# Seven block products in the output matmul of batches 2 to 6, with batch 2's products laid behind a plain chunk

## The chip, the cores and the metric

The kernel runs on one core of a Trainium2 chip. The metric is the device time of one execution in microseconds. Five engines matter: PE (TensorE, with its weight loads PEld), DVE (VectorE), ACT (ScalarE), POOL (GpSimd) and the DMA queues that SP, ACT and POOL issue to.

## The reference

Per batch and head, 32 packed rows `p` attend to `k`, `v`; then `q` attends to the packed result. The heads, side by side, are the input of a two-layer block with a cosine gate.

```python
def sm_attn(qq, kk, vv):
    s = scale * np.matmul(qq, kk.transpose(0, 1, 3, 2))
    a = np.exp(s - np.max(s, axis=-1, keepdims=True))
    a = a / (np.sum(a, axis=-1, keepdims=True) + 1e-09)
    return np.matmul(a, vv)
p_packed = sm_attn(p, k, v)             # 8 batches, 8 heads, 32 x 64
x = sm_attn(q, p_packed, p_packed)      # 8 batches, 8 heads, 576 x 64
h = x_rows @ w_in                       # 4608 x 512 @ 512 x 2048
out = (h * np.cos(h)) @ w_out           # 4608 x 2048 @ 2048 x 512
```

## The kernel before

It is a pipeline over batches. **Stage s** begins with the second attention's scores of batch s (`s2`) and lasts until those of batch s + 1. Its second part is a **slot** of 16 hidden-layer steps: four matmuls into a PSUM buffer (`psA`, three of them), a sine with bias pi/2 (so a cosine) on ACT, and the product `gT` on DVE, which gives the buffer back. Between all this, output matmuls of batch s - 1 are laid as **filler**, so that PE never waits. A batch's output has four chunks of 128 rows, and the last 64 rows of two batches make a joint chunk.

The names in the listings: `a1` holds the weights of the first attention, and a DMA transposes it to `a1T`; the **packed projection** (`pp`) multiplies `a1T` with V; the **weight product** (`PPW`) multiplies its result with `w_in`; a hidden-layer step multiplies `PPW` with `a2n`, the normalised weights of the second attention; `ot` is a PSUM buffer of the output matmuls.

```python
    def out_gen(b):                      # the filler: one matmul of 512 columns per step
        groups = [(0, 1), (2,), (3,)] if b == 0 else [(c,) for c in range(n_chunks(b))]
        for grp in groups:
            pss = {c: O.tile([128, DM], FP32, name="ot", tag="ot") for c in grp}
            ...
    for s in range(3, B):                # stage s (cut)
        fill(1000)
        set_filler(s - 1)
        if nxt:
            permute_v(s + 1)
        s2(s)
        ppw(s, 2, V)
        if nxt:
            xbar("q", s + 1)             # DMA transposes, in the order of SP's queue
        fill(10)
        if nxt:
            s1(s + 1)
            ppw(s, 3, V)
            a1_xbar(s + 1)               # transposes a1 of the next batch
            ...
        sums2(s, 1)
        normalise(s)
        fill(13)
        ...
        slot(s, [(5, lambda: pp(s + 1, engs=(ACT, ACT))), ...   # the packed projection: needs a1T
```

Only the last batch used a form with seven block products for two chunks, in `last_out`, with its partial results `o1` in the pool of V tiles (`vp`), which had two buffers.

The softmax here doesn't subtract the row's maximum and nothing guards it: scores larger than these inputs give would overflow.

## Time and profile before

247.05 us median of three runs (246.82 to 247.11). How long each stage lasts, read off PE's timeline from the first scores matmul of a stage to that of the next:

| stage | us before | filler in it |
|---|---|---|
| 2 | 25.75 | batch 1: 80 matmuls of 512 columns |
| 3 | 25.22 | batch 2: 64 |
| 4 | 28.42 | batch 3: 80 |
| 5 | 25.22 | batch 4: 64 |
| 6 | 28.35 | batch 5: 80 |

Sixteen matmuls at 0.216 us are 3.46 us; 28.42 - 25.22 is 3.2. So from stage 3 on a stage's length follows its count of filler, which is what a full PE looks like. Stage 2, laid out otherwise, is shorter than stage 4 with the same count.

### The profile page before, as it was taken

How to read it: one execution, taken by the hardware profiler on the slowest of the kernel's cores; microseconds unless marked ns; L12 is line 12 of the kernel's file. 1: busy time of each engine (PE TensorE's matmuls, PEld its weight loads, DVE VectorE, ACT ScalarE, POOL GpSimd, SP SyncE). 2: the span in 40 equal slices, each digit the busy share in tenths (PEclk: the TensorE clock that was granted, in tenths of full speed). 3: DMA queues.
4: the chain of work that ended last, by engine and by line, in shares of the span. 5: the costliest groups of instructions: out<-in, count | busy, mean ns of one | idle time of the engine just before them, and what ended most of it. 6: DMA issues, size and time to landing. Idle time of an engine off the chain costs nothing.

```text
span 245.3 us, 5164 instructions
## 1 busy us (share of the span) xinstructions
PE 235.1 (96%) x2061; PEld 134.2 (55%) x2061; DVE 171.0 (70%) x262; ACT 169.4 (69%) x283; POOL 84.7 (35%) x91
## 2 busy tenths in 40 slices
PE   8888799999999999999999999999999999999993
PEld 3454374566545654575446554565456554566682
DVE  2449987677667877678857666678667865788542
ACT  2359789877666887888876777887777774876000
POOL 8252543241310454005411305020529960099000
PEclk9999999999999999999999999999999999999999
DMA  6999999999899989998999994999381111301332
GB/s 89 202 203 206 204 207 227 201 241 156 179 189 186 199 171 217 224 203 135 220 196 202 155 232 83 178 172 200 82 169 43 43 45 43 86 3 44 84 88 86
DMA packets 64391, 37.36 MB, mean 152 GB/s; under 512 B 36880, under 2 KB 59920, under 8 KB 64368
## 3 DMA queue, kind: packets, MB, share of 16 engines
q0 software_dynamic: 23152, 18.75, 50.0%
q1 hardware_dynamic: 40784, 18.09, 35.4%
q8 instruction: 16, 0.26, 0.4%
q10 hardware_dynamic: 432, 0.20, 0.4%
q14 instruction: 7, 0.06, 0.1%
HBM read 37.22 MB, written 9.44 MB: 190 GB/s over the span
## 4 chain that ended last, share of the span: by engine, by line
PE 80%; DMA 11%; DVE 3%; ACT 3%; issue 1%; POOL 1%; DVEq 0%; POOLq 0%
PE ot L387 43%; PE psA L256 22%; DMA w_in_bf<-in_moe_w_in_dram 7%; PE ot L360 5%; DMA vbf<-in_v_dram 3%; PE psA L207 3%; DVE gT L263 2%; PE psA L129 2%; ACT cosT L260 2%; PE psA L183 2%; PE psA L233 1%; PE ot L370 1%; ACT ppT L75 1%; DVE vp L77 0%; PE psA L166 0%
## 5 line engine op out<-in xcount | busy, mean ns | idle before, releaser
L387 PE MATMUL ot<-w_out_bf,gT 128*128 128x512 bf16 x448 | 119.3, 380 | 0.0
L263 DVE TENSOR_TENSOR gT<-psA,cosT 128x576 bf16<-128x576 f32 x128 | 93.8, 756 | 28.6 <-ACT cosT L260 27.8
L260 ACT ACTIVATE cosT<-psA 128x576 bf16<-128x576 f32 x128 | 82.4, 652 | 24.6 <-PE psA L256 22.1
L256 PE MATMUL psA<-a2n,PPW 128*128 128x288 bf16 x512 | 83.8, 286 | 1.4 <-DVE gT L263 0.4
L256 PEld LDWEIGHTS <-PPW 128*128 128x128 bf16 x512 | 49.3, 98 | 34.8 <-issue 4.1
L387 PEld LDWEIGHTS <-gT 128*128 128x128 bf16 x448 | 41.6, 98 | 35.7 <-issue 6.5
L77 DVE CAST PPW<-psA 128x1024 bf16<-128x1024 f32 (+1 forms) x23 | 26.9, 1175 | 11.6 <-PE psA L207 11.5
L267 POOL COPY joint<-gT 128x512 bf16<-128x512 bf16 x16 | 10.0, 627 | 38.3 <-DVE gT L263 38.3
L77 POOL COPY vp<-vbf 96x3072 bf16<-96x3072 bf16 x7 | 19.3, 2750 | 6.3 <-DMA vbf<-in_v_dram 6.3
L243 DVE SCALAR_TENSOR_TENSOR a2n<-a2u,r,lns 128x576 bf16<-128x576 bf16 x16 | 12.3, 813 | 7.3 <-ACT lns L241 7.3
L235 ACT ACTIVATE lns<-psA 128x576 f32<-128x576 f32 x16 | 10.2, 650 | 7.1 <-PE psA L233 6.5
L140 ACT ACTIVATE a<-psA 128x576 bf16<-128x576 f32 x16 | 10.3, 647 | 6.7 <-PE psA L129 6.7
L77 DVE COPY osb<-ot 128x512 f32<-128x512 f32 x18 | 12.4, 691 | 2.1 <-PE ot L387 1.4
L387 PE MATMUL ot<-w_out_bf,joint 128*128 128x512 bf16 x48 | 13.0, 379 | 0.0
L225 ACT ACTIVATE a2u<-psA,rs 128x576 bf16<-128x576 f32 x16 | 11.0, 738 | 1.4 <-PE psA L129 1.3
L608 POOL COPY gate<-kT 1x1 bf16<-1x1 bf16 x3 | 0.5, 180 | 32.4 <-DMA kT<-kbf 32.4
L75 ACT CAST ppT<-psA 64x128 bf16<-64x128 f32 x24 | 6.2, 260 | 6.7 <-DVE ppT L77 5.9
L207 PE MATMUL psA<-w_in_bf,ppT 64*32 64x512 bf16 x224 | 10.1, 380 | 0.0
L425 PE MATMUL ot<-wz 128*128 128x512 bf16 x25 | 8.9, 496 | 1.2 <-DVE wz L436 1.2
L241 ACT ACTIVATE lns<-lns 128x576 f32<-128x576 f32 x16 | 10.0, 676 | 0.0
L314 POOL TENSOR_TENSOR S<-gT 128x256 bf16<-128x256 bf16 x8 | 5.4, 671 | 12.5 <-DVE gT L263 12.5
L84 POOL DMA_DIRECT2D vbf<-in_v_dram x8 | 6.2, 775 | 6.4 <-DVE vp L77 4.4
(94 smaller groups left out, 216.4 us busy)
## 6 DMA issues: line engine op xcount, KB each, us to landing
kbf<-in_k_dram POOLq DMA_DIRECT2D x8, 576.0 KB, 12.8
vbf<-in_v_dram POOLq DMA_DIRECT2D x8, 576.0 KB, 8.0
qbf<-in_q_dram POOLq DMA_DIRECT2D x8, 576.0 KB, 9.9
out_dram<-osb SPq DMA_DIRECT2D x22, 192.0 KB, 2.8
out_dram<-osb SPq DMA_DIRECT2D x24, 128.0 KB, 2.4
w_in_bf<-in_moe_w_in_dram POOLq DMA_DIRECT2D x4, 512.0 KB, 17.2
w_out_bf<-in_moe_w_out_dram POOLq DMA_DIRECT2D x4, 512.0 KB, 20.8
out_dram<-osb SPq DMA_DIRECT2D x22, 64.0 KB, 2.2
```

The source lines that it names most:

```text
L77: eng.tensor_copy(out=out, in_=in_)
L140: ACT.activation(out=a1[b % 2][:, y, :, 0:TP].rearrange("p (e m) x -> p e m x", e=2), in_=ps[y][:, :, 0:HS].rearrange("p e (m x) -> p e m ...
L207: nc.tensor.matmul(ps[y][32 * x:32 * x + 32, :], ppT[b % 2][r, 2 * x + y, :], w_in_bf[r, x, n * 512:(n + 1) * 512], start=True, stop=True)
L225: ACT.activation(out=a2u[b][:, y].rearrange("p (e x) -> p e x", e=2), in_=ps[y][:, :, 0:HS], func=AF.Exp, scale=rs1[b][:, y:y + 1])
L235: ACT.activation(out=lns[b][:, y].rearrange("p (e x) -> p e x", e=2), in_=ps[:, :, 0:HS], func=AF.Ln)
L241: ACT.activation(out=lns[b][:, y], in_=lns[b][:, y], func=AF.Exp, scale=-1.0)
L243: V.scalar_tensor_tensor(out=a2n[b][:, y], in0=a2u[b][:, y], scalar=r1[b][:, y:y + 1], in1=lns[b][:, y], op0=ALU.mult, op1=ALU.mult)
L256: nc.tensor.matmul(ps[:, e, 0:HS], PPW[b][:, y, fc * 128:(fc + 1) * 128], a2n[b][:, y, e * HS:(e + 1) * HS], start=(y == 0), stop=(y == 1))
L260: ACT.activation(out=csv, in_=ps[:, :, 0:HS], func=AF.Sin, bias=PI_HALF)
L263: V.tensor_tensor(out=gT[b][:, fc, :].rearrange("p (e x) -> p e x", e=2), in0=ps[:, :, 0:HS], in1=csv, op=ALU.mult)
L360: nc.tensor.matmul(ps[:, i], lhs[:, kp, :], rhs[:, kp, :], start=kp == 0, stop=kp == 7)
L387: nc.tensor.matmul(pss[c], w, w_out_bf[:, fc, :], start=(fc == 0), stop=(fc == NFC - 1))
```

## The change

The intent: fewer PE cycles. Chunks 0 and 1 of batches 2 to 6, seen as a 2 x 2 block matrix product, take seven block products (56 matmuls of 256 columns) and additions in place of eight (32 of 512). The sums of blocks of `gT` (`S`) are made on POOL in the slot, those of weight blocks (`T`) once, the last of them ahead of the loads of slot 2; DVE puts the products together from PSUM. The joint chunks are dealt as halves, one to each batch from 1 to 6. Batches 3 to 6 begin with the products; batch 2 has a plain chunk ahead of them. To make room, the pool of V tiles has one buffer in place of two.

```diff
-    vp_pool = ctx.enter_context(tc.tile_pool(name="vp", bufs=2))
+    vp_pool = ctx.enter_context(tc.tile_pool(name="vp", bufs=1))
...
+    def pair_gen(b, p):
... (operands cut)
+        def then2(ps):
+            plus(o1[:, 0:3:2, :], ps, m1)
+        def then7(ps):
+            plus(u3, ps[:, 0], o1[:, 2])
+            plus(o2[:, 0], ps[:, 1], u3)
+        def then5(ps):
+            plus(o2[:, 1], ps[:, 0], u3)
+            store(o2, 2 * p + 1)
+            plus(o1[:, 2], ps[:, 0], o1[:, 2])
+            plus(o1[:, 1], ps[:, 1], o1[:, 2])
+            store(o1, 2 * p)
+        for names, then in (((1,), lambda ps: copy(V, m1, ps[:, 0])), ((2, 6), then2), ((7, 4), then7), ((5, 3), then5)):
... (8 matmuls of 256 columns for each product)
+    def joints_of(b):
+        return [(b - (b + 1) % 2, (b + 1) % 2)] if 0 < b < B - 1 else []
...
     def out_gen(b):
+        joints = [joint_half(j, i, store_half(j)) for j, i in joints_of(b)]
+        if b == FIRST:                       # FIRST = 2
+            yield from direct_gen(b, ((2,),))
+            yield from pair_gen(b, 0)
+            yield from direct_gen(b, ((3,),))
+            for g in joints:
+                yield from g
+            return
+        if b > FIRST:
+            yield from pair_gen(b, 0)
+            for g in joints:
+                yield from g
+            yield from direct_gen(b, ((2,), (3,)))
+            return
...
+            elif s >= FIRST and fc in (7, 11, 15):
+                S_sums(s, 0, G, *{7: (0, 4), 11: (4, 6), 15: (6, 8)}[fc])
...
-            fill(quota - first if first != quota else quota)
+            fill_halves(quota - first if first != quota else quota)
```

Cut are: Ln and Exp left in PSUM from batch 3 on, the small scale on ACT, PPW in quarter tiles, and the last batch's second set of sums, moved between its additions.

## The prediction

> **What bounds the kernel now.** I read the page first: its busy shares, its tenths, and the chain that ended last.
>
> ```profile
> span 245.3 us, 5164 instructions
> PE 235.1 (96%) x2061; PEld 134.2 (55%) x2061; DVE 171.0 (70%) x262; ACT 169.4 (69%) x283; POOL 84.7 (35%) x91
> PE 80%; DMA 11%; DVE 3%; ACT 3%; issue 1%; POOL 1%; DVEq 0%; POOLq 0%
> ```
>
> PE is named in both. A busy share alone proves little, because a matmul's recorded time holds its latency. So I asked the waits view for PE alone from 96 to 225 us: it lists none. The DMA part of the chain is the first 30 us (the loads of V and of the first weights), which the change does not touch. Next, the windows of four slots; a slot is the stretch of 16 hidden-layer steps of a batch, between which output matmuls of the batch before are laid ("filler").
>
> ```profile
> core 0: us, PE busy (x) PEld busy (x) DVE busy (x) ACT busy (x) POOL busy (x), PEclk, DMA share, GB/s
> 103.65:118.60 14.95, 14.87 (x131) 9.48 (x129) 12.00 (x17) 12.44 (x22) 3.10 (x5) 1.00 1.01 179
> 128.88:148.50 19.62, 19.62 (x161) 11.53 (x166) 13.97 (x19) 14.66 (x25) 3.25 (x6) 1.00 1.03 185
> 157.40:172.00 14.60, 14.53 (x129) 9.27 (x127) 11.81 (x16) 12.11 (x22) 2.32 (x4) 1.00 0.99 180
> 182.50:202.00 19.50, 19.50 (x153) 11.49 (x150) 13.98 (x19) 14.61 (x25) 16.96 (x7) 1.00 0.17 47
> ```
>
> PE is full in all of them; DVE and ACT have 2.5 to 6 us to spare in each; slots alternate between short ones (27 filler matmuls) and long ones (43), because a joint chunk goes with every second batch. POOL is nearly free, except where it makes the weight sums T. What a matmul really costs is read from the chain in order of time, where pieces follow each other without a gap (start, duration, what):
>
> ```profile
> 126.08 2.81 PE ot L387 x13
> 226.24 3.45 PE ot L370 x16
> 229.70 8.87 PE ot L360 x80
> 238.57 1.92 PE ot L360 x16
> ```
>
> A 512-column matmul takes 2.81/13 = 3.45/16 = 0.216 us. The 256-column ones of the seven-product form, which the kernel already uses for the last batch, take 8.87/80 = 0.111 us, small waits for a PSUM buffer included; two stretches of eight in the timeline take 0.87 us, so 0.109 without a wait.
>
> **What the Trainium skill says.** (1) "TensorE: Matmul & The Clock Gate", section "Back-to-back issue gap": N/2.4 + 2.5 ns for a warm isolated gap, so 215.8 ns for 512 columns and 109.2 ns for 256. The trace agrees (216 and 109); the smaller sustained figure of that section, 131 ns for 512, does not appear here. (2) The same page, section "LDWEIGHTS (loading the stationary operand)": a load of 128 columns takes 128/1.2 = 107 ns. The trace has 98 ns. Both are under 109, so the loads, which double in number, should stay hidden, barely. (3) "SBUF — State Buffer", section "Who interferes with whom": a DVE instruction with at most one SBUF input, outside the two-port modes, does not contend with GpSimd. The trace agrees: the gT product (one PSUM, one SBUF input) takes 745 to 759 ns all through, also in the 16 us in which POOL makes T. The additions of the change also read PSUM and one SBUF tile.
>
> **The change, part by part.**
>
> PE work. For each of batches 2 to 6, chunks 0 and 1 cost 2 x 16 = 32 matmuls of 512 columns now; seven products of 8 matmuls of 256 columns replace them. Per batch: 32 x 0.216 = 6.91 against 56 x 0.109 = 6.10, so 0.81 us saved, 4.0 us for five. The three joint chunks become six halves: 48 x 0.216 = 10.37 against 96 x 0.109 = 10.46, 0.1 us lost. Together 3.9 us saved, if each comes off PE's full queue.
>
> Balance. The filler in halves is 136 for each of batches 2 to 6 (56 + 64 + 16), against 64 or 80 full ones in turn. With 62 halves ahead of the slot and 10 kept, 64 halves remain for each of slots 3 to 7: PE needs 16 x 0.49 + about 7.0 + 0.8 (packed projection) + 1.1 (two weight products) = 16.7 us, against about 14.3 us of ACT (16 cosines at 0.69 start to start, 4 small casts 1.07, one PPW cast 1.01, copies 0.37 and 0.58, one scale 0.2). So these stay PE's. A short slot has some 0.4 us of PE gaps now (14.94 us for 14.5 of work in the first window): three such gaps should shrink, 0.6 us gained at most, part of it lost in the former long slots.
>
> Slot 2 pays for it: its filler falls from 80 to 72 full matmuls, so from 28 in the slot to 20. PE's work there falls by 1.73 us to 14.0, but ACT's is 11.0 + 1.07 + 1.01 + 2 x 0.58 + 0.2 = 14.4 us. I charge 0.8 us of the saving as lost.
>
> DVE. Per pair: a copy of 256 columns 0.41, an addition of 512 0.69, and five of 256 at 0.42, 3.2 us, less one or two output copies of 0.69; the small scale (0.175 us) moves to ACT. About 8 us more in all, 179 busy, beside PE. The instruction order shows the two a2n products between the third and fourth addition groups: the fourth product ends 4 halves (0.44 us) after the second sum's matmuls, its two additions take 0.85, and the first a2n product can't start before Ln and Exp (1.3 us), so the additions fit ahead of it. The rest has 2 us of filler before it delays a PSUM buffer. No cost.
>
> Ln and Exp work in PSUM from batch 3 on, which keeps two of three PSUM buffers until the a2n products, where nothing but the hidden layer asks for them: no cost.
>
> POOL. Per batch 12 sums: 8 of 128x256 at 0.67 us, and 4 of 128x512, which I estimate at 1.17 us from 0.67 and the 4.06 us of 128x2048 by a straight line: 10.0 us, so about 135 us busy in all. Where the loads are issued late (their gate opened at 110.75 and 133.7 us, inside slots 3 and 4), POOL runs the sums late: last S2 near 123.4 us against its use near 123.5. I charge 0.3 us. The weight sum T3 (4.06 us) goes where POOL waited 4.52 us for kT ahead of the loads of slot 2: hidden.
>
> Tail. The pool of V tiles now has one buffer, and the last batch's two output tiles o1 live in it. In the timeline before, the first pair's last addition ends at 236.4 us and its store lands some 2.1 us later, near 238.6; the second pair's first addition, at 237.83 us now, writes the other buffer. With one buffer it must wait for that store: 0.8 us, and PE's (1,4) product waits for its PSUM bank in turn. Nothing hides it. I charge 0.9 us. The sums S of the second pair are moved between additions, and DVE has the 1.5 us for them: no cost.
>
> Sum: -3.9 + 0.8 (slot 2) + 0.3 (POOL) + 0.9 (tail) - 0.4 (balance) = -2.3 us; the time is 247.05 - 2.3 = 244.75. I put it at 244.6.
>
> **The rivals.**
>
> A: PE gives all of it. PE has no waits in the middle, for it; the slot-2 sum on ACT and the single o1 buffer against. It would make 247.05 - 3.9 - 0.5 = 242.7.
>
> B: POOL becomes a bound. Its 10 us of sums come behind the loads in one queue, and the third product (S2) waits for the last four. If PE waits about 1 us in each of five batches, all is given back: 247 to 248. For it, the late gate; against it, slack of about 1 us in the later batches, where DMA idles at 148 to 150 us and the gate follows the stage.
>
> C: DMA becomes a bound. Its share is 1.0 until 178 us, and loads, transposes and gate form a loop of about 23.3 us (gate at 87.19, 110.75, 133.70). Stages take 25.2 and 28.4 us now and about 26 after: still above 23.3. If it bit, I would lose another 1 us, 246.
>
> D: the additions on DVE delay gT or a2n, since DVE is in order: 0.3 us per batch, 1.5 us in all: 246. The spare 2.5 to 6 us per slot speak against it.
>
> **Range and chances.** Between A and the sum of B, C and D I hold 243.0 to 246.3. Faster by over 2% means under 242.1, which needs more than PE's whole saving: 0.03. Slower by over 2% means over 252: 0.01. Within 2%: 0.96.
>
> **What would show it.** (1) PE's matmul rows: 56 per batch at 0.109 us start to start in the chain; if 0.12, LDWEIGHTS binds. (2) Slots 3 to 7 of equal length near 16.7 us, slot 2 near 14.7 with ACT fuller than PE. (3) In PE's waits, no POOL tile S; if S shows, B holds. (4) In the tail, the second o1 addition waiting on a store of the first, about 0.8 us. (5) gT products still near 756 ns while POOL makes S. The prediction is wrong if the stages ahead of slots lengthen (a2n behind additions), or if the gap between the gates is what the stage lasts.

## The result

The changed kernel took 247.29 us (median of four runs, 246.86 to 247.37), the kernel before 247.08 (246.82 to 247.28) in the same session. The ratio is 1.0005, with a 95% interval of 0.9988 to 1.0023: the same time. A ratio here is the mean time of one kernel's fast runs over that of the other's of the same rounds, so not quite the ratio of the medians quoted. Executions over 1.5% slower than the fastest of the same kernel are left out of the means. The class was foreseen, 244.6 us and the range up to 246.3 were not. The traced execution took 246.86 us, the lowest of the four.

The page of the changed kernel: PE has 3.6 us less to do, POOL 48 us more, and the span is 0.3 us shorter.

```profile
span 245.0 us, 5618 instructions
PE 231.5 (94%) x2229; PEld 150.5 (61%) x2229; DVE 176.3 (72%) x280; ACT 169.5 (69%) x293; POOL 132.3 (54%) x150
PE 70%; DMA 18%; DVE 5%; ACT 3%; POOL 2%; issue 2%; DVEq 0%; POOLq 0%
```

The share of DMA in the chain rose from 11% to 18%, that of DVE from 3% to 5%: the path no longer runs over PE alone. PE's waits say where. From 96 to 225 us there were none before; the three below, in the middle and at the end, are new:

```profile
PE psA L189 <- DMA a1T<-a: 1.0, 1, 1.0
PE psA L212 <- DVE gT L279: 0.3, 1, 0.3
PE ot L454 <- DVE o L422: 0.8, 1, 0.8
```

L189 is the packed projection, L212 the weight product of the next batch, L454 a product of the last batch. The first two lie in stage 3. The windows of stages 3 and 4 (length, then busy time of PE, PEld, DVE, ACT, POOL with their instructions, granted clock, DMA share, GB/s), first before, then changed:

```profile
94.81:120.03 25.22, 25.14 (x221) 14.06 (x220) 18.96 (x27) 20.51 (x35) 6.46 (x7) 1.00 1.12 198
120.03:148.45 28.42, 28.42 (x238) 15.58 (x238) 19.46 (x27) 21.31 (x36) 6.51 (x8) 1.00 1.11 189
```

```profile
94.37:122.04 27.67, 26.38 (x261) 18.12 (x260) 20.62 (x32) 20.65 (x36) 20.08 (x25) 1.00 1.15 187
122.04:148.03 25.99, 25.99 (x262) 17.93 (x261) 20.24 (x31) 20.84 (x37) 16.02 (x19) 1.00 1.14 190
```

Stage 4 became 2.4 us shorter, and PE is busy in all of it. Stage 3 became 2.5 us longer, and PE idles 1.3 us of it, though both stages hold nearly the same PE instructions now (x261 and x262).

Both kernels were profiled again, unedited, in a later session. All four executions by stage, with the change in PE work that the prediction's own figures give (0.216 us per full matmul, 0.109 per half: 56 + 16 halves and 32 full against 64 or 80 full):

| part of the span | before | changed | before, again | changed, again | change in PE work |
|---|---|---|---|---|---|
| up to stage 1 | 38.47 | 38.34 | 38.42 | 38.41 | 0 |
| stage 1 | 30.59 | 31.31 | 30.82 | 30.99 | 0 |
| stage 2 | 25.75 | 24.72 | 25.61 | 24.73 | -1.7 |
| stage 3 | 25.22 | 27.67 | 25.23 | 27.08 | +0.9 |
| stage 4 | 28.42 | 25.99 | 28.41 | 25.99 | -2.5 |
| stage 5 | 25.22 | 25.91 | 25.23 | 25.91 | +0.9 |
| stage 6 | 28.35 | 25.90 | 28.34 | 25.90 | -2.5 |
| stage 7, to its joint chunk | 24.06 | 25.01 | 24.06 | 25.02 | +0.9 |
| from there to the end | 19.22 | 20.15 | 19.28 | 20.17 | 0 |
| span | 245.3 | 245.0 | 245.4 | 244.2 | -4.0 |

The row before the last is good to 0.05 us only, since the span is printed to 0.1 us.

Stages 4 to 7 give what was predicted, or a little more. The saving is eaten in stages 1, 2, 3 and after the last stage.

### The profile page after: what moved, and what is told of

It is laid out like the page before. It is cut to its first block, busy times and chain, and to the rows that moved or that the text cites. A ratio compares the mean times of both kernels' runs of the same rounds, so it can differ in the third digit from the quotient of the medians.

```text
span 245.0 us, 5618 instructions
## 1 busy us (share of the span) xinstructions
PE 231.5 (94%) x2229; PEld 150.5 (61%) x2229; DVE 176.3 (72%) x280; ACT 169.5 (69%) x293; POOL 132.3 (54%) x150
## 4 chain that ended last, share of the span: by engine, by line
PE 70%; DMA 18%; DVE 5%; ACT 3%; POOL 2%; issue 2%; DVEq 0%; POOLq 0%
PE ot L348 21%; PE psA L272 18%; PE ot L402 12%; DMA w_out_bf<-in_moe_w_out_dram 9%; DMA w_in_bf<-in_moe_w_in_dram 7%; PE ot L454 5%; PE ot L336 4%; DVE gT L279 3%; PE psA L212 3%; DMA a1T<-a 2%; ACT cosT L276 2%; PE psA L189 2%; PE psA L133 2%; PE ot L464 1%; PE psA L243 1%
## 5 line engine op out<-in xcount | busy, mean ns | idle before, releaser
L348 PE MATMUL ot<-w_out_bf,gT 128*128 128x512 bf16 x288 | 80.1, 380 | 0.2 <-DMA w_out_bf<-in_moe_w_out_dram 0.2
L348 PEld LDWEIGHTS <-gT 128*128 128x128 bf16 x288 | 26.5, 98 | 20.5 <-issue 4.9
L317 POOL TENSOR_TENSOR S<-gT 128x256 bf16<-128x256 bf16 (+1 forms) x38 | 30.3, 797 | 9.9 <-DVE gT L279 9.7
L402 PEld LDWEIGHTS <-S 128*128 128x128 bf16 x160 | 15.3, 98 | 3.2 <-POOL S L317 1.0
L402 PE MATMUL ot<-T,S 128*128 128x256 bf16 x120 | 16.6, 273 | 0.0
L317 POOL TENSOR_TENSOR S<-S,gT 128x256 bf16<-128x256 bf16 (+1 forms) x19 | 15.1, 797 | 1.5
L317 POOL TENSOR_TENSOR S<-gT,S 128x256 bf16<-128x256 bf16 (+1 forms) x19 | 15.1, 797 | 0.0
L336 PE MATMUL ot<-w_out_bf,joint 128*128 128x256 bf16 x96 | 13.9, 273 | 0.0
L402 PEld LDWEIGHTS <-gT 128*128 128x128 bf16 x120 | 11.4, 98 | 3.0 <-issue 1.3
L212 PE MATMUL psA<-w_in_bf,ppT 64*32 64x512 bf16 x224 | 10.3, 381 | 0.3 <-DVE gT L279 0.3
L245 ACT ACTIVATE psA<-psA 128x576 f32<-128x576 f32 x10 | 6.3, 635 | 5.8 <-issue 2.7
```

The lines of the kernel that those rows point to most:

```text
L212: nc.tensor.matmul(ps[y][32 * x:32 * x + 32, :], ppT[b % 2][r, 2 * x + y, :], w_in_bf[r, x, n * 512:(n + 1) * 512], start=True, stop=True)
L317: eng.tensor_tensor(out=out, in0=in0, in1=in1, op=op)
L336: nc.tensor.matmul(ps, joint[b // 2][:, fc, :], w_out_bf[:, fc, cols], start=(fc == 0), stop=(fc == NFC - 1))
L348: nc.tensor.matmul(pss[c], gT[b][:, fc, c * 128:(c + 1) * 128], w_out_bf[:, fc, :], start=(fc == 0), stop=(fc == NFC - 1))
L402: nc.tensor.matmul(ps[:, i], lhs[:, kp, :], rhs[:, kp, :], start=kp == 0, stop=kp == 7)
```

## The experiments

Medians in us, all results correct. Experiments 1 to 4 ran on one chip, 7 to 12 on another, 13 and 14 on a third; "before" is the median of the kernel before on the same chip. By the margin of 2% every one of them is "the same" as the kernel before; the intervals show the smaller differences.

| run | median | before | ratio, 95% interval |
|---|---|---|---|
| e1_o1_own | 246.11 | 246.93 | 0.9962 (0.9950 to 0.9975) |
| e2_pp_late | 245.30 | 246.93 | 0.9930 (0.9917 to 0.9942) |
| e3_a1_first | 246.63 | 246.93 | 0.9978 (0.9965 to 0.9991) |
| e4_plain | 248.90 | 246.93 | 1.0075 (1.0061 to 1.0089) |
| e7_o1_pp | 244.54 | 247.22 | 0.9894 (0.9880 to 0.9909) |
| e8_o1_pp_joint | 244.18 | 247.22 | 0.9876 (0.9861 to 0.9891) |
| e9_o1_pp_quota | 244.22 | 247.22 | 0.9878 (0.9865 to 0.9892) |
| e10_all | 244.18 | 247.22 | 0.9887 (0.9864 to 0.9910) |
| e11_slot2_pp | 244.31 | 247.16 | 0.9893 (0.9872 to 0.9915) |
| e12_first3 | 246.90 | 247.16 | 0.9982 (0.9969 to 0.9995) |
| e13_changed_again | 247.11 | 247.00 | 0.9994 (0.9974 to 1.0015) |

All edits are to the changed kernel. The theory at the start had three parts: the single V buffer costs 0.9 us at the end; late arrival of the transposed a1 costs the 1.0 us that PE's wait shows in stage 3; the rest of that stage is DVE. The main rival for stage 3: the wait on a1T hides another one, so that an earlier a1T would not give the time back.

**e1: the last batch's o1 in buffers of its own.**

```diff
-            o1 = vp_pool.tile([128, 3, 256], FP32, name="o1", tag="vp")
+            o1 = o_pool.tile([128, 3, 256], FP32, name="osb1", tag="osb1", bufs=2)
```

> Only change: the two output tiles o1 of the last batch come from a pool with two buffers. Theory (the tail's single buffer costs 0.9 us, on PE's path): 246.4 us, against 247.3 changed and 247.1 before; the tail from the first matmul of the last products to the end goes from 21.0 to 20.1 us, and PE's 0.81 us wait for the DVE addition is gone. Rival (the second pair's addition waits for something else, for instance for the moved S sums): the time stays at 247.3 and the tail at 21.0.

The median was 246.11 us. The end part fell from 20.15 to 19.29 us, and PE's wait there went. The timelines at the second pair of the last batch, of the changed kernel and of e1 (start, duration, engine, line, what; in brackets how long the engine idled before and for what):

```profile
235.25 0.38 ACTq L417 DMA_DIRECT2D out_dram<-o  x1
237.43 0.69 DVE L422 TENSOR_TENSOR o<-ot,u 128x512 f32<-128x512 f32 x1 [2.22 <-PE ot L454]
238.18 1.03 PE L454 MATMUL ot<-T,gT 128*128 128x256 bf16 x8 [0.81 <-DVE o L422]
```

```profile
235.35 0.38 ACTq L417 DMA_DIRECT2D out_dram<-osb  x1
236.70 0.69 DVE L422 TENSOR_TENSOR osb<-ot,u 128x512 f32<-128x512 f32 x1 [1.38 <-PE ot L454]
237.44 1.03 PE L454 MATMUL ot<-T,gT 128*128 128x256 bf16 x8
```

In the changed kernel the addition starts 2.2 us after the store of the first pair's o1 was issued, and 0.2 us after it landed (at 237.21); PE waits 0.81 us for the addition; in e1, where this store is issued 0.1 us later, it starts 0.73 us earlier, and PE doesn't wait. The theory holds. The profile puts the idle time of DVE down to PE; what it really waited for, the buffer still being stored, shows only when the buffer is given.

**e2: the packed projection three steps later in slot 3.**

```diff
-        slot(s, [(2, lambda: scaled(s + 1)), (5, lambda: pp(s + 1, engs=(ACT, ACT))), ...
+        slot(s, [(2, lambda: scaled(s + 1)), (8 if s == 3 else 5, lambda: pp(s + 1, engs=(ACT, ACT))), ...
```

> Only change: in slot 3 the packed projection of batch 4 comes after step 8 and not after step 5. Theory (stage 3 lasts 27.67 us and not 25.9 because PE stands before this projection until the transposed a1 has landed at 108.7 us): PE's wait goes, stage 3 falls to about 26.2 us, the time to about 246.0. Rival (stage 3 is long because the DVE additions of batch 2's pair and the POOL sums delay its slot): stage 3 stays above 27.2, the time at 247.2.

Stage 3 fell from 27.67 to 26.16 us, by 1.51, more than the wait on a1T, which landed as late as in the changed kernel (5.6 us after its issue). The later place avoids the wait on a1T and any other at step 5 alike, so this run can't tell them apart. No PE wait is left in the stage, and 26.16 is near the 25.9 to 26.0 of stages 4 to 6:

```profile
110.23 0.86 PE L189 MATMUL psA<-a1T,vp 96*128 96x64 bf16 x24
113.51 0.62 PE L212 MATMUL psA<-w_in_bf,ppT 64*32 64x512 bf16 x16
```

**e3: the transpose of a1 ahead of that of q, in stage 3 alone.** This tells the late a1T from a second wait under it: a1T comes early, the projection stays at step 5.

```diff
-        if nxt:
+        if nxt and s != 3:
             xbar("q", s + 1)
...
             a1_xbar(s + 1)
+            if s == 3:
+                xbar("q", s + 1)
```

> Only change: in stage 3 the transpose of a1 is issued ahead of the transpose of q on the same queue. Theory (late landing of a1 is a matter of its place behind q in a full DMA queue): it lands some 3 us earlier, PE's wait goes, stage 3 falls to about 26.2 us, the time to about 246.0. Rival (the DMA engines are full with the loads of batch 4 and 5, so that the place in the queue doesn't matter): it lands at 108 us or later again, and the time stays near 247.

Neither outcome came. a1T was issued at 98.93 us and landed 5.2 us later, at 104.1, long before its use at 108, as the theory had it. Yet stage 3 still took 27.09 us and not 26.2. The wait on a1T turned into another:

```profile
108.08 0.86 PE L189 MATMUL psA<-a1T,vp 96*128 96x64 bf16 x24 [0.42 <-DVE gT L279]
114.68 0.41 PE L212 MATMUL psA<-w_in_bf,ppT 64*32 64x512 bf16 x8 [0.26 <-DVE gT L279]
```

So the rival holds for the larger part. Late a1T costs 27.67 - 27.09 = 0.6 us; behind it lies a wait for a PSUM buffer that DVE has not given back, worth 27.09 - 26.16 = 0.9 us (0.68 of it shows as waits of PE; the rest shows as none). The timeline of the changed kernel around it shows why, first the cosine of the fourth step on ACT, then DVE:

```profile
106.25 0.65 ACT L276 ACTIVATE cosT<-psA 128x576 bf16<-128x576 f32 x1 [0.18 <-PE psA L272]
104.44 2.32 DVE L279 TENSOR_TENSOR gT<-psA,cosT 128x576 bf16<-128x576 f32 x3 [0.68 <-ACT cosT L276]
106.68 0.41 DVE L373 TENSOR_TENSOR u<-ot,osb 128x256 f32<-128x256 f32 x1
107.13 0.43 DVE L373 TENSOR_TENSOR osb<-ot,u 128x256 f32<-128x256 f32 x1
107.47 2.08 DVE L279 TENSOR_TENSOR gT<-psA,cosT 128x576 bf16<-128x576 f32 x3
...
112.87 0.41 DVE L373 TENSOR_TENSOR osb<-ot,u 128x256 f32<-128x256 f32 x1
```

L373 are the additions of batch 2's pair. A plain chunk stands ahead of that pair in the filler, so two of its four groups of additions fall inside the slot. DVE works in order: 0.84 us of additions go ahead of the fourth gT, whose PSUM buffer is what the projection then needs. The cosine of that step was ready at 106.90, and its gT started at 107.47, 0.57 us later. The last group (1.3 us) comes just ahead of the weight product. DVE is not full; the moment counts.

**e4: no pairs, all else as changed** (`FIRST = 7`).

> Only change: no pair of products before the last batch; batches 2 to 6 use plain chunks again, the joint chunks stay in halves and the balance of the slots stays. Theory (the products save 0.8 us of PE's time per batch, all of it on the path): stages 4 to 6 last 26.7 us and not 25.9, and the time is 247.3 + 3.3 to 4.0 less what the stall in stage 3 gives back (up to 1.5) = 249.5 to 251. Rival (the products save nothing on the path, since POOL, DVE or PSUM buffers take it back): stages 4 to 6 stay at 25.9, the time at 247.3 or below.

Stages 4 to 6 took 26.77, 26.70 and 26.70 us, against 25.99, 25.91 and 25.90 with pairs: 0.78 to 0.80 us saved per batch, by this PE alone, as its windows have PE busy throughout. But stage 3 is 27.22 without its pair, 0.3 of it a wait on a1T, and 27.08 in the repeat of the changed kernel with it (e13, below). So batch 2's pair, with the projection at step 5, gave next to nothing. The median missed the foreseen 249.5 to 251, since four pairs were worth having and not five.

**e12: batch 3 takes the place of batch 2** (`FIRST = 3`): batch 2 is plain, batch 3's pair stands behind a plain chunk. If the place of the pair is the cause, the waits must move to stage 4.

> The changed kernel with batch 2 left plain, so that batch 3's pair is now the one that comes behind a plain chunk, in stage 4. Theory (a pair behind a plain chunk has its additions inside the slot, where DVE holds up gT and so the PSUM buffer of the projection; 0.9 us, apart from the late a1): stage 4 grows from 26.0 to 26.7 to 27.0 us, stage 3 is near the 27.2 of the run without pairs; the time about 248.2. Rival (the additions cost nothing and stage 3 was long only because of the late a1): stage 4 stays at 25.9 to 26.0, the time at 247.5 or below.

They did: the same two waits, of the same length within 0.01 us. Stage 4 grew from 25.99 to 27.01 us, and no such wait was left in stage 3:

```profile
135.19 0.86 PE L189 MATMUL psA<-a1T,vp 96*128 96x64 bf16 x24 [0.42 <-DVE gT L279]
141.80 0.41 PE L212 MATMUL psA<-w_in_bf,ppT 64*32 64x512 bf16 x8 [0.25 <-DVE gT L279]
```

A pair behind a plain chunk costs 1.0 us with the projection at step 5, and saves 0.8. The foreseen median was missed: 246.90 us and not 248.2, on the rival's side of the line (247.5). It is the waits and the length of stage 4 that tell, not the median; stage 3, plain here, took 26.81 us in place of the 27.2 foreseen, with a1T landing after 4.5 us and no wait on it. That is 0.3 less than the 27.08 of e13 with batch 2's pair and no wait on a1T: the same loss from the other side. Batch 2's pair ahead of its plain chunks was not tried, so whether its sums would be ready there is open.

**e7: e1 and e2 together.**

> Both repairs together: own buffers for o1 and the packed projection of slot 3 after step 8. Theory (two separate losses, of 0.86 us in the tail and 1.5 us in stage 3): they add, 244.4 us; the tail near 19.3 us, stage 3 near 26.2. Rival (one hides a part of the other): above 245.0.

Their gains add: 0.38% and 0.70% by themselves, 1.06% together, 244.54 us. The traced execution (245.07 us) is the slowest of the four; what it lost is told under e10.

**e8: e7, with both halves of the first joint chunk in batch 1's filler**, so that the short slot 2 has more PE work and stage 3 less.

```diff
-        return [(b - (b + 1) % 2, (b + 1) % 2)] if 0 < b < B - 1 else []
+        return [(1, 0), (1, 1)] if b == 1 else [(b - (b + 1) % 2, (b + 1) % 2)] if 2 < b < B - 1 else []
```

> The two repairs, and the second joint half of batches 0 and 1 goes back from the filler of stage 3 to that of stage 2 (16 matmuls of 256 columns, 1.74 us of PE). Theory (slot 2 has too little filler: ACT and DVE set its length and PE has some 0.7 us of gaps more than before): stage 2 grows by 1.0 us to about 25.7, stage 3 falls by 1.7 to about 24.4, the time falls 0.7 below that of the two repairs, to 243.7. Rival (slot 2 is bound by PE): stage 2 grows by 1.7, the time stays at 244.4.

The first half of the expectation held: stage 2 took 1.74 us more of PE work and lasted 25.35 us, 0.6 more than the 24.73 of e2, e3 and e13, where its projection doesn't wait (e7's own 25.44 holds such a wait). So it has PE time to give. But stage 3 fell by 0.51 us alone, from 26.15 to 25.64, and not by the 1.7 of 16 half matmuls: with fewer matmuls between them, its steps waited on gT again. The two changes nearly cancel. 244.18 us lies below all four runs of e7 (244.45 to 245.07), but the two intervals against the kernel before overlap.

**e9: e7, with the filler of slots 1 and 2 dealt in whole matmuls**, as the kernel before did.

```diff
+            if s < FIRST:
+                quota = 2 * ((left // 2 * sum(weight[:fc + 1])) // sum(weight)) - (left + keep - filler[1])
...
-                    first = quota // 2
+                    first = quota // 4 * 2 if s < FIRST else quota // 2
```

> The two repairs, and the filler of slots 1 and 2 is dealt in whole matmules as before (the order of the matmuls in slot 1 is then that of the kernel before). Theory (0.3 us of slot 1 were lost to the other dealing): the time from the first step of slot 1 to the start of stage 2 goes from 25.0 back to 24.7 us, the total to 244.1. Rival (POOL's first weight sum in slot 1, or the scale on ACT, takes it): it stays at 25.0, the total at 244.4.

In slot 1 all filler is full matmuls, but the quota counts halves, which shifts where each goes. From its first step to stage 2 slot 1 took 24.68 us before, 25.0 changed, and 24.67 here. The 0.33 us are the dealing. With 244.22 us, 1.2% below the kernel before, it beats both kernels, if by less than 2%. e8 and e10 are as fast (244.18), so which of the three to keep is not decided by the times.

**e10: e8 and e9 together.**

> All four edits. If each of the theories holds: 247.2 - 0.86 - 1.5 - 0.7 - 0.3 = 243.4 to 243.8 us, that is 1.3 to 1.5% under the kernel before. If slot 2 is bound by PE and slot 1 by POOL: 244.4.

A miss: 244.18 us with the widest spread (243.88 to 245.92). Its profile shows a wait of 0.5 us on a1T at L189 in stage 2, the pattern of stage 3 again. It is not new with these edits. The lines of e7, e9 and e10:

```profile
84.91 0.86 PE L189 MATMUL psA<-a1T,vp 96*128 96x64 bf16 x24 [0.76 <-DVE gT L279]
84.48 0.86 PE L189 MATMUL psA<-a1T,vp 96*128 96x64 bf16 x24 [0.54 <-DMA a1T<-a]
84.63 0.86 PE L189 MATMUL psA<-a1T,vp 96*128 96x64 bf16 x24 [0.46 <-DMA a1T<-a]
```

e7's wait is put down to gT, but a1T landed at 84.78, 0.13 us before the projection began, as in e9 and e10 (84.35 and 84.50). e1 and e4 have such a wait too (0.24 and 0.42). In both profiles of the kernel before this transfer landed 0.1 to 0.2 us ahead of its use: it had no slack there either. So the profiled length of stage 2 (24.7 to 25.4 over the runs with the same filler in it) depends on this landing, and two runs can't be compared by it alone.

**e11: e9, with the projection of slot 2 two steps later.**

> Own o1 buffers, slot 3's projection after step 8, whole-matmul dealing, and in slot 2 the projection after step 9 and not 7. Theory (slot 2 is short of PE work, so ACT and DVE set its length whatever the order): stage 2 stays at 24.7 to 25.4 us, the time at 244.2. Rival (slot 2 loses because its projection comes while a1 of batch 3 is still being transposed and PSUM waits on gT): stage 2 falls to about 24.2, the time to 243.6.

The projection now waits 0.12 us in place of e9's 0.54, and stage 2 of the profiled execution is 24.82 in place of 25.21; the median didn't follow (244.31 and 244.22). And 24.82 is not below the 24.72 of the changed kernel, where the projection doesn't wait. So the 0.7 us that slot 2 loses there are not a wait for the projection. Which of ACT and DVE paces that slot is not settled.

**e13 and e14: the changed kernel and the kernel before again, unedited.**

> The changed kernel once more, unedited, for a second trace and a closer ratio. Theory (the loss by the additions in slot 3 and by the tail is fixed, the wait for the late a1 is a matter of when a transfer lands): the time within 0.3% of the kernel before; the tail near 20.15 us again and the 0.25 us wait of the weight product in slot 3 again; the landing of a1 in stage 3 anywhere from 3.9 to 5.7 us after its issue, and stage 3 accordingly 27.0 to 27.9. Rival (the late a1 belongs to the change): it lands after 5.6 us again.

> The kernel before once more, unedited, for a second trace. Theory: slot 1 takes 24.7 us from its first step to the start of stage 2 again (the 0.3 us of the dealing is fixed), stages 3 and 4 take 25.2 and 28.4 again, whatever the landing of a1 (3.9 to 5.6 us). Rival: with a1 landing after 5.6 us stage 3 grows by the same 0.7 us as in the changed kernel.

e14 took 247.13 us. Slot 1 took 24.68 us and stages 3 and 4 took 25.23 and 28.41, as foreseen; a1T landed after 3.9 us again, so its rival was not put to the test.

For e13: 0.9994. But the profiled execution took 246.07 us, and the table above shows it 1.2 us shorter in span than the kernel before in the same session, where the first had been 0.3. Two places differ from the first profile of the changed kernel. In stage 3 a1T landed 3.9 us after its issue in place of 5.6, and PE's wait is that of e3 with e3's length of stage (27.08 and 27.09):

```profile
108.03 0.86 PE L189 MATMUL psA<-a1T,vp 96*128 96x64 bf16 x24 [0.42 <-DVE gT L279]
114.63 0.41 PE L212 MATMUL psA<-w_in_bf,ppT 64*32 64x512 bf16 x8 [0.26 <-DVE gT L279]
```

And ahead of slot 1 a wait of 0.24 us on w_out in the first profile is absent. So 0.8 us of the first profile (0.59 in stage 3, 0.24 here) was the arrival of two transfers, which changes between executions of one and the same kernel. Whether the change makes a late arrival more likely is taken up below. The five fast runs lie at 246.07, 246.09, 246.78, 247.45 and 247.47; only the first was traced, so what the slower ones lost is likely the same, but not shown.

## Why the prediction was wrong

The prediction's sum gives 244.75; that it was put at 244.6 is not accounted for. Its terms against the two pairs of profiles, by the stage table:

| term | predicted | first pair | second pair |
|---|---|---|---|
| PE work | -3.9 | -3.95 | -3.95 |
| slot 2 | +0.8 | +0.70 | +0.85 |
| POOL | +0.3 | 0 | 0 |
| end | +0.9 | +0.93 | +0.89 |
| balance, stages 4 to 7 | -0.4 | -0.08 | -0.06 |
| stage 3 beyond its work | - | +1.51 | +0.91 |
| start and stage 1 | - | +0.59 | +0.16 |
| sum | -2.3 | -0.3 | -1.2 |

**The step that failed** is "DVE": "the additions fit ahead of it", "The spare 2.5 to 6 us per slot speak against it", and with it "No cost". It was worked out on a pair that begins the filler, and is right for batches 3 to 6: PE has no wait from 122 to 225 us. Batch 2's pair, which the change's own words set apart, stands behind a plain chunk; there the additions hold gT at the two moments at which PE needs a PSUM buffer. That costs 0.9 to 1.0 us (e3, e12, e13). Rival D named the mechanism, but spread it over five batches at 0.3 us and put it aside by an average. The measured 247.29 us lies in the 247 to 248 of rival B (POOL as a bound), but that is luck: no matmul of PE waits for a sum S (three of its weight loads do, 1.0 us in all, while PE stays busy).

**A second step was missing.** The slack of the transposed a1 was never read. Before, a1T landed in stage 3 at 103.15 + 3.9 = 107.05 us, and the projection began at 108.01: 1.0 us of slack.

```profile
103.15 1.47 SPq L156 DMA_TRANSPOSE a1T<-a  x1
108.01 0.86 PE L183 MATMUL psA<-a1T,vp 96*128 96x64 bf16 x24
```

The time from issue to landing in stage 3, before and changed:

```profile
a1T<-a SPq DMA_TRANSPOSE x1, 3.9
```

```profile
a1T<-a SPq DMA_TRANSPOSE x1, 5.6
```

With 1.7 us more, it came after its use: 1.0 us of wait, of which 0.6 net, as the DVE wait lies under it. Why it takes longer in some executions is open. The kernel before had 3.9 in both of its profiles. In the eleven of the changed kernel and its variants with the same order of transposes it took 3.9 to 4.0 twice (e9, e13), 4.5 to 4.9 three times (e4, e10, e12) and 5.6 to 5.8 six times (the first, e1, e2, e7, e8, e11). So the change probably has a part in it; what part is not shown. The prediction had transfers as rival C, but as a bound on a stage's length, and never asked for the slack of a single one.

**A third, small one:** "Balance" counted the filler in halves but did not ask where slot 1's full matmuls would fall by that count: 0.33 us (e9).

**What was right:** the size of the saving (0.78 to 0.80 us per batch in e4, 0.81 predicted), that the added weight loads (56 for 32 in a pair) stay hidden, that slots 4 to 6 come out equal (17.44, 17.36 and 17.36 us from the first step to the next stage), the length lost in slot 2 (0.70 of 0.8), the single buffer at the end with its mechanism (0.93 of 0.9, e1), the gT products unmoved beside POOL (757 ns median with POOL busy 132 us), and that 2% would not be reached. In slot 2 the length came as said, the reason less so: ACT is busy 12.0 us of its 14.5 and PE 14.3, so "ACT fuller than PE" did not show, and what paces that slot is open (e11). The sum of 14.4 us for ACT was misread: it counts 16 cosines at 0.69 us from start to start, idle time included, where one takes 0.65; the prediction's own first window had ACT busy 12.44 of 14.95 us. That the 0.8 us came true is thus in part luck. Two sizes were off: POOL's sums kept PE from nothing (0.3 charged), and the balance gave 0.1 in place of 0.4. These two cancel.

## What to carry to other kernels

When the same work is added to several iterations, look where it falls in the in-order stream of each helper engine for every iteration that is laid out otherwise than the rest: spare time over a stage says nothing about the moment at which a full engine needs a buffer back. Before moving work, read the slack of each transfer to its first use, and give a margin to one that has a microsecond; two one-line moves (a later projection, a second buffer) were worth more here than the saving of one whole batch. A wait seen in the trace may cover another, so take it away by itself and see what the stage gives back.

## What the Trainium skill lacked or had wrong

- "TensorE: Matmul & The Clock Gate", section "Back-to-back issue gap": it calls 131 ns the sustained spacing of 512-column matmuls in a real kernel. Here the sustained spacing is 216 ns (13 in 2.81 us), and 109 ns for 256 columns, which is the formula that the page keeps for isolated ones.
- "DMA: Bandwidth & Descriptors", section "Latency and other measured facts": 261 GB/s for a DMA transpose with a non-contiguous middle dimension would be 1.5 us for the 393 KB of a1 (an estimate from the page's rate). That transpose, in stage 3, took 3.9 to 5.8 us from issue to landing over the runs, with a DMA share of 1.15 in the stage, so the page is not shown wrong; what it lacks is the time of a transpose while loads are under way, and its spread between executions, which cost 0.6 us here.
- "GPSIMD Engine Reference", section "3.1 Elementwise — side-by-side cycle accounting": its measured `tensor_tensor` time is for fp32 alone. Here the bf16 sums took 668 ns for 128x256, 1156 for 128x512 and 4065 for 128x2048, so 1.9 ns per element and a fixed 0.18 us.
- No page has how additions in DVE's in-order stream, with DVE 75% busy in the stage (20.62 of 27.67 us), hold the matmuls of another product through the count of PSUM buffers: 0.42 + 0.25 us of visible waits and 0.9 to 1.0 us of the stage.
